# Top-k attention and GELU MLP in f32: the product of the last rows by column halves, scores of 512 in one matmul, preparation pieces spread in a slot

## The chip, the cores and the metric

One core of a Trainium2 chip runs the whole program. The metric is device time in microseconds (us), median of three runs. A separate, profiled execution gives the profile; in it, times are counted from the first instruction. The engines are TensorE (PE; its weight loads are listed as PEld), VectorE (DVE), ScalarE (ACT), GpSimd (POOL) and SyncE (SP), which issues most of the DMAs.

## The reference

Attention with a top-k mask, then an MLP with exact GELU. Shapes: batch 8, 8 heads, 576 rows, head size 64; the MLP goes 512 to 2048 to 512 for all 4608 rows. All of it is f32.

```python
scores = scale * np.matmul(q, k.transpose(0, 1, 3, 2))
kth = np.partition(scores, -32, axis=-1)[..., -32:-31]
scores = np.where(scores >= kth, scores, -1000000000.0)
attn = np.exp(scores - np.max(scores, axis=-1, keepdims=True))
attn = attn / (np.sum(attn, axis=-1, keepdims=True) + 1e-09)
x = np.matmul(attn, v)              # (B,H,S,D) -> (B*S, H*D)
h = x @ w_in
g = 0.5 * h * (1.0 + erf(h / sqrt(2)))
return g @ w_out
```

## The kernel before

**Items.** Heads are taken in pairs; a pair's q, k and v lie side by side in 128 columns (head e=0 in 0 to 63, e=1 in 64 to 127). The 576 rows of a head are four tiles of 128 (t = 0 to 3) and a last tile of 64 (t = 4, NM in the code). An item is one tile of both heads of a pair. The last 64 rows of two neighbouring pairs share an item, so a batch has 16 main items and 2 last items, 144 items in all. Even batches end with their last items and odd ones begin with them, so four last items come in a row: 16 to 19, 52 to 55, 88 to 91 and 124 to 127.

**Slots.** The loop at L616 works on several items at a time. Its pass n, called slot n here, issues in this order: `scores(n+2)`, `attend(n-3)` (product with v, for every second main item and every last item), the transposes of item n-2, both softmax halves of item n-1, and top-k of item n. Between them it puts pieces of the MLP (`mlp(1)`), eight in most slots. Every engine has its own queue and runs it in exactly the order in which the code issues; nothing reorders it.

**Scores** (L281). For a main item there is one matmul for the last 64 columns of both heads (L291) into the PSUM tile `t_ps`, and four (L295) into `s_ps`: two heads by two halves of 256 columns. The heads use rows 0 to 63 and 64 to 127 of the array. ACT copies both with a scale (L299, L300). For a last item four small matmuls (L305, 64 weight columns by 64) and four of 512 (L316) do the same.

**Softmax.** DVE finds the top 32 (L342, L345). POOL makes `neg` and `bias` of them (L357, L360). ACT applies Prelu with a steep slope (L381) and Exp with a running sum `den` (L382), once for each head e. POOL adds 1e-9 to `den` (L374), DVE takes its reciprocal `rden` (L368), inside top-k of the next item, and POOL normalises both heads (L393).

**Transposes** (L399) come as three pieces: `tails` (L410, or L415 for a last item) with the last 64 columns of both heads, then `main(0)` and `main(1)` with four 128x128 transposes each (L428). ACT copies each result out of PSUM (L411 or L420, L435).

**Product** (L441). For main items, 2 x 5 matmuls of 256 columns (L459) with 64 weight columns for each head: head e=0 writes PSUM partitions 0 to 63, e=1 writes 64 to 127. One ACT copy moves the result into `xT` (L464). For last items, 2 pairs x 5 matmuls (L469) use all 128 weight columns and 128 moving columns; a half of what they compute belongs to another head and isn't used, and two ACT copies take the other half (L475).

**Preparation** (L238). For each pair, ten 128x128 transposes of q and k (L250) come in three pieces of 4, 2 and 4, each followed by a copy into `qk`, nearly always on ACT (L254). The third (c = 0) also issues the loads of pair + 2 on SP. `slots_of` and `first` (L605 to L609) say in which slot each piece falls. Two fall in one slot in slot 2 and in slots 14, 15 and 16 of each 36.

**MLP pieces.** A piece is four matmuls' records of the first layer (L507, 256 columns) or two of the second (L543, 512 columns). They come in blocks of eight, an L2 block and an L1 block by turns. GELU_AT is 5: with the sixth piece of an L2 block ACT gets the two Gelus of the next blocks (L518). Gelu and Exp need different tables, so ACT loads a table (ACT_TABLE_LOAD) each time it goes from one to the other.

**PSUM.** `t_ps`, `o`, `tp`, `tp_t` and `tp_qk` share one tag with two buffers, used by turns in the order of issue: each new tile waits until the tile before the last has been copied out.

The order of a slot's second part is this:

```python
for piece in tr[:-1]:
    piece()
    ready[0] = n_tok[0]
    mlp(1)
...
if late:
    softmax(n - 1, 1)
add_small(n - 1)
for piece in tr[-1:] + prep_in.pop(n, []):
    piece()
    mlp(1)
```

Of the kernel before, what the change touches and what calls it, by code (L numbers as in the profile page):

```python
# [14 lines left out]
def kernel(  # L15
# [19 lines left out]
    nc = tc.nc  # L35
# [5 lines left out]
    B, H, S, D = q.shape  # L41
    P = 128
# [6 lines left out]
    TL = S - SM  # L49
    NJ = NM + 1  # L50
# [17 lines left out]
    xT = const.tile([P, KO, RING], f32, name="xT")  # L68
# [15 lines left out]
    def raw_of(n, pair):  # L84
        return raws[n][pair % len(raws[n])]

    def load(n, pair, queue=None):
        if pair >= n_pairs:
            return
        queue = queue or nc.sync  # L90
        b, h0 = pair // NP, 2 * (pair % NP)
        t, src = raw_of(n, pair), sources[n]
        for e in range(2):
            queue.dma_start(
                out=t[:, 0:NM, e, :], in_=src[b, h0 + e, 0:SM].rearrange("(t p) d -> p t d", p=P)
            )
            queue.dma_start(out=t[e * TL : (e + 1) * TL, NM, e, :], in_=src[b, h0 + e, SM:S])
# [28 lines left out]
    def unit_in(n):  # L126
        return ORDER[n - FIRST] if 0 <= n - FIRST < UNITS else None
# [66 lines left out]
    def weights_add(u):  # L194
        if u in words:
            w, _, dst = parts(u)
            d = dst.bitcast(i32)
            if on_pool(u):
                nc.gpsimd.tensor_scalar(
                    w.bitcast(i32), w.bitcast(u32), 2.0**-13, None, op0=ALU.mult  # L200
                )
            nc.gpsimd.tensor_tensor(d, d, w.bitcast(i32), op=ALU.add)
# [23 lines left out]
    def place_of(b, row):  # L226

        if row < SM:
            return b // 2 * RING + b % 2 * (SM + 2 * TL) + row
        return b // 2 * RING + SM + b % 2 * TL + row - SM  # L230
# [4 lines left out]
    KT = SM + 2 * P  # L235
# [32 lines left out]
    def spread(t, step, n):  # L268

        return bass.AP(tensor=t.tensor, offset=t.offset, ap=[list(t.ap[0]), [step, 2], [1, n]])  # L270

    def half(r, e):


        return slice((r ^ e) * TL, ((r ^ e) + 1) * TL)

    def halves(t, e, step):

        return spread(t[:, e * TL :], step + (TL if e == 0 else -TL), TL)

    def scores(i):  # L281
        if i >= N:
            return
        pair, t = items[i]
        S_of[i] = s = work.tile([P, 2 * S], f32, tag="s", bufs=5, name="s")
        s_ps = ps.tile([P, 2, 512], f32, tag="s", bufs=1, name="s_ps")
        t_ps = ps.tile([P, 512], f32, tag="tp", name="t_ps")
        if t < NM:
            qk = qk_of[pair]
            lhsT = qk[:, t * P : (t + 1) * P]  # L290
            nc.tensor.matmul(t_ps[:, 0:P], lhsT=lhsT, rhs=qk[:, SM + P : KT], start=True, stop=True)  # L291
            for c in range(2):
                for e in range(2):
                    rows = slice(e * D, (e + 1) * D)
                    nc.tensor.matmul(  # L295
                        s_ps[:, e, c * 256 : (c + 1) * 256], lhsT=lhsT[rows, :],
                        rhs=qk[rows, KT + c * 256 : KT + (c + 1) * 256], start=True, stop=True,
                    )
            nc.scalar.activation(spread(s, S + TL, SM), s_ps, func=AF.Copy, scale=scale)  # L299
            nc.scalar.activation(s[:, SM : S + TL], t_ps[:, 0:P], func=AF.Copy, scale=scale)  # L300
        else:
            for r in range(2):
                qk = qk_of[pair + r]
                for e in range(2):
                    nc.tensor.matmul(  # L305
                        t_ps[half(r, e), r * TL : (r + 1) * TL],
                        lhsT=qk[:, SM + e * TL : SM + (e + 1) * TL],
                        rhs=qk[:, SM + P + e * TL : SM + P + (e + 1) * TL],
                        start=True, stop=True,
                    )  # L310

            for r in range(2):
                qk = qk_of[pair + r]
                for e in range(2):
                    rows = slice(e * D, (e + 1) * D)
                    nc.tensor.matmul(  # L316
                        s_ps[half(r, e), r, :], lhsT=qk[rows, SM + e * TL : SM + (e + 1) * TL],
                        rhs=qk[rows, KT:], start=True, stop=True,
                    )
            s2 = s.rearrange("p (r n) -> p r n", r=2)  # L320
            nc.scalar.activation(s2[:, :, 0:SM], s_ps, func=AF.Copy, scale=scale)
            nc.scalar.activation(
                s2[:, :, SM:S], t_ps[:, 0:P].rearrange("p (r n) -> p r n", r=2),
                func=AF.Copy, scale=scale,
            )
# [115 lines left out]
    def attend(i):  # L441

        if i < 0 or i >= N:
            return False
        pair, t = items[i]
        b, at = divmod(pair, NP)
        if t < NM and t % 2 == 0:
            return False
        pt = pt_now[0]
        o = ps.tile([P, 512], f32, tag="tp", name="o")  # L450
        n, row = (2 * P, (t - 1) * P) if t < NM else (TL, SM)
        tok = place_of(b, row)
        assert read[0] >= tok + n - RING
        c = slice(tok % RING, tok % RING + n)
        if t < NM:
            vt = raw_of("v", pair)
            for j in range(NJ):
                for e in range(2):
                    nc.tensor.matmul(  # L459
                        o[e * D : (e + 1) * D, 0:n], lhsT=vt[:, j, e, :],  # L460
                        rhs=pt[:, e * NM + j if j < NM else 2 * NM, :],
                        start=(j == 0), stop=(j == NJ - 1),
                    )
            nc.scalar.copy(out=xT[:, at, c], in_=o[:, 0:n])  # L464
        else:
            for r in range(2):
                vt = raw_of("v", pair + r)
                for j in range(NJ):
                    nc.tensor.matmul(  # L469
                        o[:, r * P : (r + 1) * P], lhsT=vt[:, j].rearrange("p e d -> p (e d)"),  # L470
                        rhs=pt[:, r, j, :], start=(j == 0), stop=(j == NJ - 1),
                    )
            for e in range(2):
                r = slice(e * D, (e + 1) * D)
                nc.scalar.copy(out=xT[r, at : at + 2, c], in_=halves(o[r, 0 : 2 * P], e, P))  # L475

        if t == (NM if b % 2 == 0 else NM - 1):
            for r in range(2 if t == NM else 1):
                load("v", pair + r + NP + 1)
        if at == (NP - 1 if t < NM else NP - 2):  # L480
            assert n_tok[0] == tok
            n_tok[0] = tok + n
        return True
# [93 lines left out]
    def mlp(n):  # L577
        for _ in range(n):
            if done[0] >= len(pieces) or pieces[done[0]][0] > ready[0] or left[0] == 0:
                return  # L580
            pieces[done[0]][1]()
            done[0] += 1
            left[0] -= 1
# [26 lines left out]
    prep_in = {}  # L610
    for pair in range(2, n_pairs):
        b, p = divmod(pair, NP)
# [3 lines left out]
    for n in range(ahead):  # L616

        left[0] = 7 if START < n < START + 2 * NP else 8
        weights_add(unit_in(n))
        scores(n + 2)  # L620
        product = attend(n - 3)
        late = n > START + 1
        mlp(1)
        tr = transposes(n - 2)
        if product and done[0] < len(pieces) and pieces[done[0]][0] > ready[0]:

            for piece in tr[:1]:
                piece()
            tr, ready[0] = tr[1:], n_tok[0]
        softmax(n - 1, 0)  # L630
        mlp(1)
        if not late:
            softmax(n - 1, 1)
        mlp(1)
        for piece in tr[:-1]:
            piece()
            ready[0] = n_tok[0]
            mlp(1)
        ready[0] = n_tok[0]
        if late:  # L640
            softmax(n - 1, 1)
        add_small(n - 1)
        for piece in tr[-1:] + prep_in.pop(n, []):
            piece()
            mlp(1)
        mlp(left[0])
        if n < N:
            top_k(n, {3: lambda: inverse(n - 1)})
        else:
            inverse(n - 1)  # L650
        threshold(n)
        normalise(n - 1)

        weights_sign(unit_in(n))
        weights_size(unit_in(n + 1))
        if n >= FIRST:
            load_weights(n + 2)
        if n <= NP:
            load("v", n)
# [36 lines left out]
```

## Time and profile before

| what | value |
|---|---|
| median of 3 runs | 1690.68 us (1690.24 to 1690.70) |
| profiled execution, its own time | 1691.79 us |
| its span, first to last instruction | 1690.0 us |
| mean granted TensorE clock | 0.977 |
| L469 matmuls, 320 records | 40.0 us busy |
| L295 matmuls, 1024 records | 156.5 us busy |
| L459 matmuls, 1280 records | 155.1 us busy |
| L507 and L543 matmuls | 554.7 and 549.1 us busy |
| L250 transposes, 320 records | 61.2 us busy |

In the profile, the busy time of a group is the union of its instructions, so matmuls that run side by side are counted once. A matmul's listed duration is longer than the distance to the next one, since they are pipelined; the cost of one is read from start to start. An f32 matmul of the program appears as two records, a transpose as one. The lines of a timeline give start, length, engine, line, operation, out<-in, the array rows and columns that are used ("128*64"), the shape of the moving operand and the number of merged records, and in brackets the engine's idle time before and what ended it.

### The profile page before, as it was taken

What the parts mean: (1) busy time and instruction counts of PE and PEld (TensorE: products, weight loads), DVE (VectorE), ACT (ScalarE), POOL (GpSimd) and SP (SyncE); (2) the same over time, 40 slices, a digit from 0 to 9 for tenths busy, and PEclk for the clock granted to TensorE, in tenths of its full rate; (3) what the DMA queues carried; (4) which work ended last, traced back from release to release, by engine and by line L of the source; (5) the groups of instructions that cost most, each with busy time, mean ns of one, the idle gap of its engine ahead of it and who ended that gap; (6) DMA issues with size and microseconds to landing.
All of it is one profiled execution on the core that took longest, in us unless ns stands there. A gap on an engine that the chain in (4) does not pass through costs nothing.

```text
span 1690.0 us, 24403 instructions
## 1 busy us (share of the span) xinstructions
PE 1611.4 (95%) x8480; PEld 1093.3 (65%) x8480; DVE 1428.8 (85%) x3042; ACT 1188.1 (70%) x2147; POOL 662.5 (39%) x764
## 2 busy tenths in 40 slices
PE   5659899999999999999999999999999999999999
PEld 3336567676666667676666667676666666766665
DVE  6999798998889888998889888898889988899900
ACT  5778677777777777777777777777777777777730
POOL 3668743333333332333333333333333333333410
PEclk8669999999999999999999999999999999999999
DMA  6422210001100011002110111001110000000000
GB/s 158 135 91 98 78 48 9 11 18 35 29 27 15 27 29 41 1 13 49 25 31 1 35 36 41 1 14 28 32 46 1 27 15 15 21 1 13 7 13 13
DMA packets 126715, 56.10 MB, mean 33 GB/s; under 512 B 117888, under 2 KB 117888, under 8 KB 126592
## 3 DMA queue, kind: packets, MB, share of 16 engines
q1 hardware_dynamic: 125056, 52.16, 11.6%
q0 software_dynamic: 320, 2.10, 0.4%
q8 instruction: 67, 1.10, 0.3%
q14 instruction: 56, 0.46, 0.1%
q10 hardware_dynamic: 1216, 0.30, 0.1%
HBM read 45.08 MB, written 9.44 MB: 32 GB/s over the span
## 4 chain that ended last, share of the span: by engine, by line
PE 87%; ACT 5%; DVE 5%; POOL 1%; issue 1%; DMA 1%; SPq 0%; ACTq 0%; POOLq 0%
PE h_ps L507 29%; PE y_ps L543 28%; PE o L459 8%; PE s_ps L295 7%; PE tp L428 7%; DVE top L342 2%; PE o L469 2%; DVE rest L345 2%; PE tp_qk L250 2%; PE t_ps L291 2%; ACT s L382 1%; PE tp_t L410 1%; PE s_ps L316 1%; ACT s L381 1%; ACT L518 1%
## 5 line engine op out<-in xcount | busy, mean ns | idle before, releaser
L342 DVE MAX8 top<-rest 128x8 f32<-128x576 f32 x864 | 610.8, 750 | 0.0
L507 PE MATMUL h_ps<-xT,w_in_sb 128*128 128x256 f32 (+1 forms) x2560 | 554.7, 362 | 6.8 <-DMA xT<-in_moe_w_out_dram 4.9
L543 PE MATMUL y_ps<-w_out_sb,g 128*128 128x512 f32 x1152 | 549.1, 599 | 0.0
L393 POOL TENSOR_SCALAR s<-s,rden 128x576 f32<-128x576 f32 x288 | 493.5, 1723 | 0.8 <-issue 0.4
L507 PEld LDWEIGHTS h_ps<-xT,w_in_sb 128*128 128x128 f32 x2560 | 430.1, 191 | 69.4 <-issue 18.4
L345 DVE MATCH_REPLACE8 rest<-top,rest 128x576 f32<-128x576 f32 x576 | 424.3, 746 | 0.0
L374 POOL TENSOR_SCALAR den<-den 128x2 f32<-128x2 f32 x144 | 32.0, 222 | 868.7 <-ACT s L382 868.2
L543 PEld LDWEIGHTS y_ps<-w_out_sb,g 128*128 128x128 f32 x1152 | 195.4, 191 | 166.0 <-issue 164.6
L299 ACT ACTIVATE s<-s_ps 128x1024 f32<-128x1024 f32 x128 | 131.5, 1027 | 173.2 <-PE s_ps L295 153.0
L382 ACT ACTIVATE s<-s,bias 128x576 f32<-128x576 f32 x288 | 223.3, 776 | 13.2 <-ACT s L381 0.4
L381 ACT ACTIVATE s<-s,neg 128x576 f32<-128x576 f32 x288 | 223.7, 777 | 0.7 <-POOL neg L357 0.2
L435 ACT COPY pt<-tp 128x512 f32<-128x512 f32 x256 | 146.8, 575 | 98.2 <-PE tp L428 97.6
L345 DVE MATCH_REPLACE8 rest<-top,s 128x576 f32<-128x576 f32 x288 | 212.1, 746 | 0.0
L342 DVE MAX8 top<-s 128x8 f32<-128x576 f32 x288 | 202.2, 745 | 5.1 <-ACT s L300 5.1
L428 PEld LDWEIGHTS tp<-ident,s 128*128 128x128 f32 x1152 | 145.9, 144 | 93.3 <-issue 58.1
L428 PE MATMUL tp<-ident,s 128*128 128x128 f32 x1152 | 177.7, 278 | 6.4 <-ACT pt L411 6.4
L368 DVE RECIPROCAL rden<-den 128x2 f32<-128x2 f32 x144 | 23.6, 164 | 169.8 <-POOL den L374 169.5
L295 PE MATMUL s_ps<-qk 64*128 64x256 f32 x1024 | 156.5, 427 | 0.4 <-ACT s L299 0.4
L459 PE MATMUL o<-pt,raw_v 128*64 128x256 f32 x1280 | 155.1, 389 | 1.8 <-ACT pt L435 1.8
L459 PEld LDWEIGHTS o<-pt,raw_v 128*64 128x64 f32 x1280 | 87.5, 139 | 69.5 <-issue 15.1
L295 PEld LDWEIGHTS s_ps<-qk 64*128 64x128 f32 x1024 | 94.1, 198 | 24.3 <-issue 2.5
L518 ACT ACTIVATE g<-h_ps 128x512 f32<-128x512 f32 x144 | 78.7, 595 | 38.8 <-PE h_ps L507 38.0
(65 smaller groups left out, 1106.7 us busy)
## 6 DMA issues: line engine op xcount, KB each, us to landing
raw_q<-in_q_dram SPq DMA_DIRECT2D x64, 128.0 KB, 2.4
raw_v<-in_v_dram SPq DMA_DIRECT2D x64, 128.0 KB, 2.4
out_dram<-y SPq DMA_DIRECT2D x32, 256.0 KB, 2.2
raw_k<-in_k_dram SPq DMA_DIRECT2D x62, 128.0 KB, 2.4
w_out_sb<-in_moe_w_in_dram SPq DMA_DIRECT2D x12, 511.8 KB, 4.8
w_out_sb<-in_moe_w_out_dram SPq DMA_DIRECT2D x10, 511.8 KB, 3.9
w_out_sb<-in_moe_w_in_dram POOLq DMA_DIRECT2D x4, 511.8 KB, 7.7
words<-in_moe_w_out_dram SPq DMA_DIRECT2D x4, 511.8 KB, 6.5
```

What stands on the lines that cost most here:

```text
L295: nc.tensor.matmul(s_ps[:, e, c * 256 : (c + 1) * 256], lhsT=lhsT[rows, :], rhs=qk[rows, KT + c * 256 : KT + (c + 1) * 256], start=True, s ...
L299: nc.scalar.activation(spread(s, S + TL, SM), s_ps, func=AF.Copy, scale=scale)
L342: nc.vector.max(st["top"][:, e, 8 * r : 8 * r + 8], cur[e])
L345: nc.vector.match_replace(rest[:, e], st["top"][:, e, 8 * r : 8 * r + 8], cur[e], LOWEST)
L381: nc.scalar.activation(s, s, func=AF.Prelu, bias=st["neg"][:, e, 1:2], scale=1.0, alpha=STEEP)
L382: nc.scalar.activation(s, s, func=AF.Exp, bias=st["bias"][:, e : e + 1], scale=1.0, accum_out=st["den"][:, e : e + 1],)
L393: nc.gpsimd.tensor_scalar(s, s, st["rden"][:, e : e + 1], None, op0=ALU.mult)
L428: nc.tensor.transpose(tp[:, j * P : (j + 1) * P], s[:, first + j * P : first + (j + 1) * P], ident)
L435: nc.scalar.copy(out=dst, in_=tp.rearrange("p (j n) -> p j n", j=NM))
L459: nc.tensor.matmul(o[e * D : (e + 1) * D, 0:n], lhsT=vt[:, j, e, :], rhs=pt[:, e * NM + j if j < NM else 2 * NM, :], start=(j == 0), stop= ...
L507: nc.tensor.matmul(h_tile(u)[:, i, :], lhsT=w_in_sb[:, ko, f * P : (f + 1) * P], rhs=xT[:, ko, c0 : c0 + n], start=(ko == 0), stop=(ko == ...
L543: nc.tensor.matmul(y_of[sub], lhsT=g_of[u][:, i, sub * P : (sub + 1) * P], rhs=w_out_sb[:, f, :], start=(f == 0), stop=(f == FT - 1),)
```

## The change

There are three parts. The product of the last rows calls one matmul for each head, with 64 weight columns and the 64 moving columns of this head, into the partitions of this head; one copy replaces two. The scores of a main item take one matmul of 512 columns for each head instead of two of 256. In a slot with two or more preparation pieces and three transpose pieces, the first preparation piece is issued behind the first transpose piece, and the others stay at the end.

```diff
-            for c in range(2):
-                for e in range(2):
-                    rows = slice(e * D, (e + 1) * D)
-                    nc.tensor.matmul(
-                        s_ps[:, e, c * 256 : (c + 1) * 256], lhsT=lhsT[rows, :],
-                        rhs=qk[rows, KT + c * 256 : KT + (c + 1) * 256], start=True, stop=True,
-                    )
+            for e in range(2):
+                rows = slice(e * D, (e + 1) * D)
+                nc.tensor.matmul(
+                    s_ps[:, e, :], lhsT=lhsT[rows, :], rhs=qk[rows, KT:], start=True, stop=True
+                )
...
                 for j in range(NJ):
-                    nc.tensor.matmul(
-                        o[:, r * P : (r + 1) * P], lhsT=vt[:, j].rearrange("p e d -> p (e d)"),
-                        rhs=pt[:, r, j, :], start=(j == 0), stop=(j == NJ - 1),
-                    )
-            for e in range(2):
-                r = slice(e * D, (e + 1) * D)
-                nc.scalar.copy(out=xT[r, at : at + 2, c], in_=halves(o[r, 0 : 2 * P], e, P))
+                    for e in range(2):
+                        nc.tensor.matmul(
+                            o[e * D : (e + 1) * D, r * TL : (r + 1) * TL], lhsT=vt[:, j, e, :],
+                            rhs=pt[:, r, j, half(r, e)], start=(j == 0), stop=(j == NJ - 1),
+                        )
+            nc.scalar.copy(
+                out=xT[:, at : at + 2, c],
+                in_=o[:, 0 : 2 * TL].rearrange("p (r n) -> p r n", r=2),
+            )
...
         mlp(1)
+        prep = prep_in.pop(n, [])
+        if len(prep) > 1 and len(tr) == 3:
+            tr, prep = tr[:1] + prep[:1] + tr[1:], prep[1:]
         for piece in tr[:-1]:
             piece()
             ready[0] = n_tok[0]
...
-        for piece in tr[-1:] + prep_in.pop(n, []):
+        for piece in tr[-1:] + prep:
             piece()
             mlp(1)
```

## Prediction

> **What bounds the kernel now.** I read the page first, then busy time by stretch, then the timelines of single slots (a slot is one pass of the loop at L616, dated by the first matmul of `scores`), then the waits.
>
> ```profile
> PE 1611.4 (95%) x8480; PEld 1093.3 (65%) x8480; DVE 1428.8 (85%) x3042; ACT 1188.1 (70%) x2147; POOL 662.5 (39%) x764
> PE   5659899999999999999999999999999999999999
> PE 87%; ACT 5%; DVE 5%; POOL 1%; issue 1%; DMA 1%; SPq 0%; ACTq 0%; POOLq 0%
> ```
>
> TensorE (PE) is nearly always busy and carries 87% of the chain that ended last. By stretch it is sharper:
>
> ```profile
> 41.00:228.00 187.00, 138.06 (x711) 89.35 (x712) 173.07 (x348) 145.66 (x244) 134.31 (x102) 0.82 0.31 95
> 228.00:1600.00 1372.00, 1365.52 (x7361) 936.27 (x7362) 1224.80 (x2631) 997.86 (x1830) 506.51 (x625) 1.00 0.09 22
> ```
>
> The columns are span, PE, PEld, DVE, ACT, POOL, granted clock. From 228 to 1600 us PE lacks only 6.5 us, at full clock; all of it is six gaps: three of 1.27 us (ahead of 466.74, 862.44 and 1258.14, for the data of a last `qk` piece, which the change doesn't touch) and three of 0.85 us, ahead of 598.08, 993.78 and 1389.48. So in this stretch a microsecond of PE work is a microsecond of time, while DVE has 147 us and ACT 374 us to spare. But DVE and ACT follow PE slot by slot, so a new wait of PE for ACT counts in full too.
>
> **The product of the last rows (L469).** Slot 19, and two shapes from slot 52:
>
> ```profile
> 236.23 1.14 PE L295 MATMUL s_ps<-qk 64*128 64x256 f32 x8
> 237.30 2.50 PE L469 MATMUL o<-ptt,raw_v 128*128 128x128 f32 x20
> 239.63 2.74 PE L543 MATMUL y_ps<-w_out_sb,g 128*128 128x512 f32 x6
> ```
> ```profile
> 598.08 0.45 PE L305 MATMUL t_ps<-qk 128*64 128x64 f32 x8 [0.85 <-ACT qk L254]
> 598.46 1.09 PE L316 MATMUL s_ps<-qk 64*64 64x512 f32 x8
> 599.48 2.38 PE L459 MATMUL o<-pt,raw_v 128*64 128x256 f32 x20
> 601.79 0.70 PE L507 MATMUL h_ps<-xT,w_in_sb 128*128 128x256 f32 x2
> ```
>
> Every f32 matmul of the program is two records (10 calls of L469, x20). L469 takes 237.30 to 239.63, 2.33 us: 20 steps of 0.111 and 0.11 for its first weight load. Added are 20 calls, 40 records, of 64 columns, in two column halves. L305 has just this shape: read off in narrow windows its records start in pairs, 0.058 apart (598.18, 598.24, 598.30). So 20 pairs x 0.0585 = 1.17. The change of array shape around it is read at L459: 599.48 to 601.79 is 2.31 for 10 pairs of 256 columns at 0.216 (2.16), so 0.15 for the first load and the change behind; and L507 then starts with a step of 0.32 (0.70 less one duration of 0.38) where 0.22 is usual, 0.10 more. Today L469 has no such change behind it, as L543 uses the whole array too. After: 1.17 + 0.15 + 0.10 = 1.42. **Gain 0.91 us in each of the 16 last items, 14.6 us**, all on PE, in slots 19 to 22 of each 36, which have no gap. Two ACT copies of 0.26 become one of about 0.26 (L411 moves a 128x128 tile in 0.26): 16 x 0.26 = 4.2 us of ACT, off the path, counted as nothing. What is late next there: these slots shrink from 11.7 to 10.8 us while DVE needs 9.8 (busy in each of them), so DVE keeps 1 us; the normalise of POOL ends 3.5 us ahead of the transposes that read it (250.39 against 253.91), which leaves 2.6.
>
> The unknown is whether 80 instructions (40 records and 40 weight loads) can be supplied in 1.17 us, 15 ns each. L305 does 16 at that rate, and L316's 16 follow at once. For the sequencer itself: it passed the semaphore wait ahead of L428 at 192.9 and the one ahead of L507 at 193.1, with 8 instructions between: at most 25 ns each. Bounds per item are thus 1.17 and 80 x 25 = 2.00 us. I take 1.17, since the nearest row has the very shape and part of the burst is already queued when it starts.
>
> A rule speaks against this. The Trainium skill, "TensorE: Matmul & The Clock Gate", section "Wait — 56ns, not 53.3ns?", says that with hardware decode off the sequencer spends about 62 ns on each MATMUL, which then bounds short ones. By it the product would last an estimated 40 x 62 = 2.48 us and the whole change would end near 1703 us; L305's records, 29 ns each, do not agree, though for 8 of them only.
>
> **Scores (L295).** 128 items: four pairs of 256 columns become two of 512. Now start to start (236.23 to 237.30): 1.07 = 4 x 0.216 + 0.20 for first load and change. After: 2 x 0.428 (L543's step, its 6 records end 2.74 after the first start, 5 steps and one duration of 0.60) + 0.20 = 1.06. Gain 0.007 x 128 = **0.9 us**. If the halves stopped running side by side it would cost 0.86 an item; L316 (8 records of 512, four abreast, in 1.09) excludes that. Half the weight loads go as well, hidden under matmuls: nothing.
>
> **Preparation spread.** Two pieces fall in slot 2 and in slots 14, 15, 16 of each 36. The first now runs right after the `tails` piece, so it and one more `mlp` piece stand ahead of `softmax(n-1,1)` in the order of PE and ACT. No work is added; three things move.
>
> (a) ACT makes the `qk` copy (0.59 or 0.37, next piece 1.3 later) ahead of the softmax, so `den` is 1.3 us later. In slot 50 the normalise then ends at about 590.2; `tails` of slot 51 is at 590.91. Covered by 0.7; slot 52 likewise, by 0.8. If that cover is gone it costs up to 0.6 each. The loads of `piece` c=0 that are now issued earlier go to SP, which has nothing due.
>
> (b) In slots 51, 87, 123 the extra `mlp` piece is the sixth of an L2 block, and that is the one that carries the Gelu (GELU_AT). Today:
>
> ```profile
> 592.52 0.59 ACT L435 COPY pt<-tp 128x512 f32<-128x512 f32 x1 [1.03 <-PE tp L428]
> 593.00 0.78 ACT L381 ACTIVATE s<-s,neg 128x576 f32<-128x576 f32 x1
> ...
> 594.59 0.56 ACT L435 COPY pt<-tp 128x512 f32<-128x512 f32 x1
> 595.17 1.28 ACT L518 ACT_TABLE_LOAD   x1
> ...
> 597.43 1.08 ACT L254 COPY qk<-tp_qk 128x512 f32<-128x512 f32 x2
> ```
>
> Order now: first `main` copy, softmax, second `main` copy, Gelu, both `qk` copies; the next `t_ps` needs the PSUM buffer that the first `qk` copy frees at 598.02, hence the gap of 0.85. Afterwards: `tails`, `qk`, first `main` (593.81 to 594.40), Gelu, softmax with a second table load, second `main`, `qk`; and the next `t_ps` waits for the second `main`. Slot 17 already shows that order:
>
> ```profile
> 217.92 1.28 ACT L518 ACT_TABLE_LOAD   x1
> ...
> 220.19 0.59 ACT L435 COPY pt<-tp 128x512 f32<-128x512 f32 x1
> 220.66 0.80 ACT L381 ACTIVATE s<-s,neg 128x576 f32<-128x576 f32 x1
> 221.47 1.28 ACT L382 ACT_TABLE_LOAD   x1
> ...
> 223.54 0.56 ACT L435 COPY pt<-tp 128x512 f32<-128x512 f32 x1
> ```
>
> From the table load to the end of the second copy: 224.10 - 217.92 = 6.18, less 0.47 for the copy inside, 5.7. From 594.4 that is 600.1; so the matmuls of 598.08 start at 600.15, with a gap of 3.0 us (PE is ready at 597.2). **Loss 2.1 us x 3 = 6.3.** Queued behind the late softmax on ACT are the copies that PE waits for; `den` slips from 594.76 to 599.7, so DVE's reciprocal, and DVE behind it, is 5 us late; normalise ends near 603.9, and the shifted `tails` is at 606.6, so nothing more is lost.
>
> (c) Slot 15 has its Gelu earlier and other ACT work; by the same bookkeeping the second `main` copy ends 0.8 us after the present start of slot 16: 0.8 lost. Slot 2 waits for DVE and POOL in either order: 0.
>
> **Sum:** -14.6 - 0.9 + 6.3 + 0.8 = -8.4. Against the profiled execution (1691.79; span 1690.0) that is 1683.4; the median of the runs is 1.1 lower, so **1682.3**.
>
> **Rivals.**
> B, the spreading is free: if ACT isn't in the order I derived, so that Gelu stays behind the softmax, only (a) remains, -15.5, 1675.2; with the three gaps of 0.85 gone too, 1672.6. For: PE had waits behind `qk` copies, which are now apart. Against: slot 17. Chance 0.14.
> C, the spreading costs more: the covers of 0.7 and 0.8 fail in some nine slots at 0.5 each, or DVE's 5 us come back as waits for POOL: +4.5, 1686.8 (1684 to 1689). For: margins under 1 us; against: DVE gains about 1 us a slot afterwards. Chance 0.16.
> D, slower: supply of instructions to PE in the product. At 25 ns, 2.00 us each, the gain falls to 0.08 an item: -1.3 - 0.9 + 7.1 = +4.9, 1695.6. It turns the sign from about 21 ns on (gain 0.39 an item, burst of 1.69). Against it, L305. Chance 0.12, a little over half of it at under 21 ns.
> E, the change doesn't do what it says: the halves run one behind the other, 40 x 0.0585 = 2.34, +0.25 = 2.59 against 2.33: +4.2 - 0.9 + 7.1, 1701. L305 and L459 speak against. Chance 0.04.
> My case: 0.52, 1680.5 to 1685; unnamed 0.02.
>
> **Range.** 1674.5 to 1688.5 holds my case, most of B, nearly all of C and a third of D, a little over 8 in 10. This kernel's times tell 0.2% (3.4 us) from no change. Faster by more (under 1687.3): 0.52 + 0.14 + 0.10 of C + 0.04 of D = 0.80; within: 0.06 + 0.03, 0.09; slower: 0.05 + 0.04 + 0.02 = 0.11.
>
> **What would show it.** The new product: 40 records of 128x64, first start to next piece near 1.3 us, slots 19 to 22 at 10.8 us. The gaps ahead of slots 52, 88, 124 near 3.0 us and laid to the second `main` copy, with two table loads between it and the first. L295 at 4 records, 1.06. A product of 1.7 us or more, or slots 52 without a gap, would make me wrong.

## The result and the profile after

The changed kernel takes 1686.94 us (median of 6 runs, 1686.40 to 1690.16) against 1690.69 of before: ratio 0.9983, interval 0.997 to 0.9996. It is a little faster, by 3.75 us where 8.4 were forecast. The profiled execution took 1686.40 us with a span of 1684.6, against 1691.79 and 1690.0: 5.4 less. Slot by slot this 5.4 can be told exactly, so I work with it; the median of before lies 1.1 under its profiled execution and the median of after 0.5 above.

Lines of the changed kernel have other numbers: L294 scores, L468 product of last rows, L303 and L314 scores of last items, L457 product of main items, L426 and L433 the `main` transposes and copies, L379 and L380 Prelu and Exp.

The head of its page, and busy time in the two stretches (span, PE, PEld, DVE, ACT, POOL, granted clock, DMA):

```profile
PE 1596.2 (95%) x8288; PEld 1024.6 (61%) x8288; DVE 1428.5 (85%) x3042; ACT 1181.9 (70%) x2131; POOL 662.5 (39%) x764
PE 86%; DVE 6%; ACT 5%; POOL 1%; issue 1%; DMA 1%; SPq 0%; ACTq 0%; POOLq 0%
```
```profile
41.00:228.00 187.00, 135.97 (x658) 81.28 (x656) 171.79 (x346) 145.19 (x242) 133.20 (x101) 0.82 0.30 94
228.00:1600.00 1372.00, 1358.98 (x7267) 881.00 (x7267) 1228.48 (x2639) 995.60 (x1821) 508.45 (x630) 1.00 0.09 22
```

PE is busy 15 us less in all, but from 228 to 1600 us it now lacks 13.0 us in place of 6.5. The product is where it was expected (timeline of slot 19):

```profile
236.49 1.13 PE L294 MATMUL s_ps<-qk 64*128 64x512 f32 x4
237.55 1.39 PE L468 MATMUL o<-ptt,raw_v 128*64 128x64 f32 x40
238.87 1.55 PE L543 MATMUL y_ps<-w_out_sb,g 128*128 128x512 f32 x3
```

237.55 to 238.87 is 1.32 us for 40 records. Slots 19 to 22 take 10.76, 10.80, 10.76 and 10.69 us in place of 11.68, 11.72, 11.68 and 11.61, each 0.92 less, and so do their three repeats.

Slot 51 is where time comes back. Its timeline on ACT:

```profile
590.26 0.59 ACT L433 COPY pt<-tp 128x512 f32<-128x512 f32 x1 [0.71 <-PE tp L426]
590.87 1.28 ACT L518 ACT_TABLE_LOAD   x1
592.16 1.09 ACT L518 ACTIVATE g<-h_ps 128x512 f32<-128x512 f32 x2
593.13 0.78 ACT L379 ACTIVATE s<-s,neg 128x576 f32<-128x576 f32 x1
593.92 1.28 ACT L380 ACT_TABLE_LOAD   x1
595.22 0.77 ACT L380 ACTIVATE s<-s,bias 128x576 f32<-128x576 f32 x1
...
595.99 0.56 ACT L433 COPY pt<-tp 128x512 f32<-128x512 f32 x1
```

Gelu and two table loads stand between the two `main` copies, 590.87 to 596.55, 5.7 us, and PE waits for the second. The timeline of PE after it, and the granted clock by microsecond (the column behind POOL's):

```profile
596.61 0.45 PE L303 MATMUL t_ps<-qk 128*64 128x64 f32 x8 [2.93 <-ACT pt L433]
596.99 1.09 PE L314 MATMUL s_ps<-qk 64*64 64x512 f32 x8
598.01 4.07 PE L457 MATMUL o<-pt,raw_v 128*64 128x256 f32 x20
```
```profile
597.00:598.00 1.00, 1.00 (x11) 0.20 (x8) 1.00 (x4) 0.04 (x1) 1.00 (x1) 1.00 0.00 0
598.00:599.00 1.00, 1.00 (x10) 0.68 (x8) 1.00 (x3) 0.80 (x1) 1.00 (x2) 0.64 0.00 0
599.00:600.00 1.00, 1.00 (x8) 0.52 (x6) 1.00 (x3) 0.40 (x2) 1.00 (x1) 0.50 0.00 0
...
602.00:603.00 1.00, 1.00 (x7) 0.89 (x6) 1.00 (x3) 0.88 (x2) 0.00 (x0) 1.00 0.00 0
```

The gap of 2.93 us is the one that was forecast. What follows was not: from 598.28 on TensorE gets half its clock for 3.41 us, and the main product, 2.38 us elsewhere, takes 4.07. PE counts as busy in it, so no wait and no gap shows this; it is seen in the clock, in the time of L457's matmuls and in the length of the slot. The same table by slots, for the three places:

```profile
596.61:610.76 14.15, 14.15 (x84) 10.06 (x84) 10.48 (x23) 7.33 (x15) 4.65 (x8) 0.88 0.01 1
...
992.26:1004.72 12.46, 12.46 (x83) 9.27 (x83) 10.48 (x23) 7.33 (x15) 4.64 (x8) 1.00 0.00 1
...
1386.23:1400.33 14.10, 14.10 (x83) 9.64 (x83) 10.48 (x23) 7.33 (x15) 4.64 (x8) 0.88 0.00 1
```

Same slot, same instructions: 12.46 us at full clock (as before the change), 14.15 and 14.10 where the clock was halved. The whole account against the profiled execution of before:

| where | us |
|---|---|
| product, 16 x 0.92 | -14.7 |
| gaps ahead of slots 52, 88, 124: 3 x 2.08 | +6.2 |
| half clock in slots 52 and 124: 1.69 + 1.64 | +3.3 |
| scores and what is left behind slot 19 | -0.5 |
| up to slot 19 (235.92 to 236.18) | +0.3 |
| sum | -5.4 |

### The profile page after: what moved, and what is told of

Read it like the earlier page. It is cut to its first block, busy times and chain, and to the rows that moved or that the text cites. A ratio compares the mean times of both kernels' runs of the same rounds, so it can differ in the third digit from the quotient of the medians.

```text
span 1684.6 us, 23982 instructions
## 1 busy us (share of the span) xinstructions
PE 1596.2 (95%) x8288; PEld 1024.6 (61%) x8288; DVE 1428.5 (85%) x3042; ACT 1181.9 (70%) x2131; POOL 662.5 (39%) x764
## 4 chain that ended last, share of the span: by engine, by line
PE 86%; DVE 6%; ACT 5%; POOL 1%; issue 1%; DMA 1%; SPq 0%; ACTq 0%; POOLq 0%
PE h_ps L507 30%; PE y_ps L543 28%; PE o L457 8%; PE s_ps L294 7%; PE tp L426 7%; DVE top L340 3%; DVE rest L343 3%; PE tp_qk L250 2%; PE t_ps L291 2%; PE o L468 1%; PE tp_t L408 1%; PE s_ps L314 1%; ACT s L380 1%; POOL s L391 1%; ACT L518 1%
## 5 line engine op out<-in xcount | busy, mean ns | idle before, releaser
L380 ACT ACTIVATE s<-s,bias 128x576 f32<-128x576 f32 x288 | 223.4, 776 | 13.2 <-ACT s L379 0.4
L379 ACT ACTIVATE s<-s,neg 128x576 f32<-128x576 f32 x288 | 224.0, 778 | 0.3 <-POOL neg L355 0.2
L433 ACT COPY pt<-tp 128x512 f32<-128x512 f32 x256 | 146.7, 574 | 100.6 <-PE tp L426 100.6
L426 PEld LDWEIGHTS tp<-ident,s 128*128 128x128 f32 x1152 | 146.5, 144 | 92.1 <-issue 59.2
L426 PE MATMUL tp<-ident,s 128*128 128x128 f32 x1152 | 177.8, 279 | 6.0 <-ACT pt L409 5.9
L457 PE MATMUL o<-pt,raw_v 128*64 128x256 f32 x1280 | 157.8, 394 | 1.9 <-ACT pt L433 1.8
L294 PE MATMUL s_ps<-qk 64*128 64x512 f32 x512 | 153.3, 677 | 0.4 <-ACT s L297 0.4
L457 PEld LDWEIGHTS o<-pt,raw_v 128*64 128x64 f32 x1280 | 88.6, 141 | 95.9 <-ACT qk L254 19.9
```

Source lines behind the costliest of these rows:

```text
L294: nc.tensor.matmul(s_ps[:, e, :], lhsT=lhsT[rows, :], rhs=qk[rows, KT:], start=True, stop=True)
L379: nc.scalar.activation(s, s, func=AF.Prelu, bias=st["neg"][:, e, 1:2], scale=1.0, alpha=STEEP)
L380: nc.scalar.activation(s, s, func=AF.Exp, bias=st["bias"][:, e : e + 1], scale=1.0, accum_out=st["den"][:, e : e + 1],)
L426: nc.tensor.transpose(tp[:, j * P : (j + 1) * P], s[:, first + j * P : first + (j + 1) * P], ident)
L433: nc.scalar.copy(out=dst, in_=tp.rearrange("p (j n) -> p j n", j=NM))
L457: nc.tensor.matmul(o[e * D : (e + 1) * D, 0:n], lhsT=vt[:, j, e, :], rhs=pt[:, e * NM + j if j < NM else 2 * NM, :], start=(j == 0), stop= ...
```

## The experiments

The theory: each part does what was forecast, and the spreading costs more than its gaps, since the gaps slow the clock. The rivals: the new product or scores leave slower slots behind; or the long slots come from queues on ACT or DVE.

**Product alone** (e1_product; scores and preparation as before the change).

> The product by heads alone, with the scores and the order of preparation of before. Theory (the changed kernel is short of its forecast only by what the spreading costs, gaps and a slowed clock): slots 19 to 22 of each 36 at 10.8 us in place of 11.7, 16 x 0.92 = 14.7 us less, 1676.0; the three gaps ahead of 598, 993 and 1389 stay at 0.85 and the clock stays full behind them. Rival (the new product itself leaves PE in a state in which other slots are slower, for one by its change of array shape): some of slots 52, 88, 124 are again some 1.7 us longer, and the time is 1679 or more.

1676.5 us, ratio 0.992 (0.9903 to 0.9936). Slots 55 to 58 take 10.76, 10.80, 10.76 and 10.69; the gaps stay at 0.84 to 0.85, and the clock is full from 200 us to the end. Theory holds; the new shape leaves nothing slow behind.

**Scores alone** (e2_scores; only L295 is replaced by one matmul of 512 for each head).

> The scores by one matmul of 512 alone. Forecast of the prediction: 0.007 us an item, 0.9 us less, 1689.8. By the slots of the changed kernel it is rather 0.004 us an item, 0.5 us less, 1690.2. Rival (fewer weight loads and instructions help PE elsewhere, or 512 columns in two banks hold up the copies): 2 us or more either way. No slot should differ by more than 0.02 us after 230 us.

1690.89 us, ratio 1.0001 (0.9991 to 1.001): no difference that the medians can show. In the trace slots 50 to 85 take 395.58 us in place of 395.71, 0.004 for each of their 32 main items, or 0.5 us in all.

**Spreading alone** (e3_spread).

> The spreading of the preparation alone. Theory: three gaps of 2.9 us in place of 0.85 ahead of slots 52, 88, 124, +6.2 us, and behind some of them 3.4 us of half clock, +1.7 us each: 1697 without, 1702 with all three; with some change of up to 1.5 us before 230 us. Rival (the spreading is free and the forecast was missed elsewhere): within 1 us of before. Rival (the long slots 52 are due to queues of ACT or DVE and not to the clock): they are long in all three places or in none, and the granted clock is 1.00 in them.

1703.6 us, ratio 1.0079 (1.0064 to 1.0094): alone it makes the kernel slower. The three gaps are 2.93 us, and this time all three slots behind them are slowed:

```profile
598.99:613.09 14.10, 14.10 (x84) 9.96 (x84) 10.48 (x23) 7.34 (x15) 4.65 (x8) 0.88 0.00 1
998.41:1012.51 14.10, 14.10 (x83) 9.92 (x83) 10.48 (x23) 7.35 (x15) 4.65 (x8) 0.88 0.00 0
1397.84:1411.94 14.10, 14.10 (x84) 9.92 (x84) 10.48 (x23) 7.34 (x15) 4.65 (x8) 0.88 0.00 0
```

3 x (2.08 + 1.64) = 11.2, and from slot 19 to slot 141 the profiled execution takes 11.15 us more than that of before. The medians differ by 12.9; where the other 1.7 lie isn't shown, since this profiled execution was 1.2 us shorter ahead of slot 19. ACT's and DVE's busy time in these slots is what it is in the undisturbed slot of the changed kernel (7.33 and 10.48), so queues on them are not the reason.

**Product and scores, no spreading** (e4_product_scores).

> The changed kernel without the spreading. Theory: 14.7 and 0.5 us less, 1675.5, which is faster than both kernels; gaps of 0.85 as before, clock full from 230 us on. Rival (the parts hinder one another, so that their sum is not the parts' sum): 1679 or more.

1675.6 us, ratio 0.9914 (0.9899 to 0.9929), as the theory had it, and faster than both kernels. Slots 50 to 85 take 391.9 us; the changed kernel needs 395.65 for them. The profiled executions of the two differ by 10.9 us: 6.2 by the gaps, 3.3 by the half clock, 1.5 ahead of slot 19. The medians differ by 11.3.

**The changed kernel with the Gelu one piece later** (e5_after_gelu6).

```diff
-    GELU_AT = 5
+    GELU_AT = 6
```

> The changed kernel with GELU_AT = 6, so that in slots 51, 87 and 123 the Gelu comes behind the softmax again, though the preparation is spread. Theory (the loss is the Gelu and two table loads ahead of the softmax): no gap ahead of slot 52, at most 1 us ahead of its product, which then waits for the last qk copy; no slowed clock; 1676 if nothing else moves with the constant. Rival (the loss is from the preparation pieces themselves, whatever Gelu does): gaps near 2.9 us stay, 1685 to 1690.

1672.48 us, ratio 0.9889 (0.9874 to 0.9904). With spreading and all, the gaps ahead of slots 52, 88 and 124 are gone, and so is the slow clock; ahead of the product PE waits 0.74:

```profile
592.85 0.45 PE L303 MATMUL t_ps<-qk 128*64 128x64 f32 x8
593.23 1.09 PE L314 MATMUL s_ps<-qk 64*64 64x512 f32 x8
595.06 2.38 PE L457 MATMUL o<-pt,raw_v 128*64 128x256 f32 x20 [0.74 <-ACT qk L254]
```

So it is the Gelu's place relative to the softmax that makes most of the spreading's cost, not the preparation pieces. It is also faster than expected: the three gaps of 1.27 us, which I had laid to a last `qk` piece, are gone too. There, too, the Gelu stood ahead of the `qk` copy that PE waits for (before: Gelu from 463.83, copy at 466.09, matmuls at 466.74); now the copy, at 461.20, comes ahead of the Gelu, at 462.66.

**Spreading only in slots with a product** (e6_spread_even).

```diff
-        if len(prep) > 1 and len(tr) == 3:
+        if product and len(prep) > 1 and len(tr) == 3:
```

> The changed kernel with the spreading only in slots with a product (14 and 16 of each 36), and not in slots 2 and 15, 51, 87, 123. Theory: spreading costs nothing there, the gaps are 0.85 as before, 1675.5, like product and scores without spreading. Rival (later softmax in slots 50 and 52 costs waits for the normalise of POOL, up to 0.6 us in seven slots): up to 1680.

1676.96 us, ratio 0.9913 (0.9897 to 0.993). Slots 50 and 52 take 12.46 as before: a softmax 1.3 us later costs nothing there. The covers of 0.7 and 0.8 us hold. From slot 19 to slot 141 it takes 1324.19 us, and e4_product_scores without any spreading 1324.22, so behind slot 19 the whole price of the spreading comes from slots 51, 87 and 123.

**The gap shorter by one piece** (e7_gap_short; one MLP piece moved from behind the gap to ahead of it).

```diff
+        if n > 2 * START and n % 36 in (15, 16):
+            left[0] = 9 if n % 36 == 15 else 7
```

> The changed kernel with one MLP piece (0.86 us of PE) moved from slots 52, 88, 124 to the end of the slots before them; nothing else changed. Theory (an idle stretch of nearly 3 us is what halves the clock): gaps of 2.07 us in place of 2.93, granted clock 1.00 in all three slots; 3 x 0.86 = 2.6 us less by the gaps and the share of slowed slots less: about 1682. Rival (the slow slots have another cause, such as queues behind the late softmax): two of three slots still 1.7 us long, 1684.4.

1685.97 us, ratio 0.9968 (0.9956 to 0.998). The gaps are 2.07 us, as planned, but two of the three slots are slowed again:

```profile
595.62:609.09 13.47, 13.36 (x79) 9.42 (x79) 9.80 (x22) 6.83 (x15) 4.06 (x6) 0.87 0.01 1
991.15:1002.93 11.78, 11.67 (x79) 8.62 (x79) 9.80 (x22) 6.83 (x15) 4.06 (x6) 1.00 0.01 1
1384.98:1398.41 13.43, 13.31 (x80) 9.08 (x80) 9.81 (x22) 6.84 (x15) 4.06 (x6) 0.87 0.00 1
```

My expectation that 2.07 us is too short to slow the clock was wrong. It is the clock, by its column, and not queues, since ACT and DVE are as busy in the slowed slots as in the other (6.83 and 9.80); but a shorter gap is enough. (A wait of 0.35 for POOL in slot 54 comes with the moved piece: it stands in e11_gap_shorter too, and in no other trace.)

**The gap longer by one piece** (e8_gap_long; 7 and 9 in the same two lines).

> The changed kernel with one MLP piece moved the other way, from slots 51, 87, 123 to the slots behind the gap. Theory: gaps of 3.79 us, half clock for 3.4 us behind every one of the three, each slot some 2.6 to 3.4 us longer than in before: 2.6 us more by the gaps and 1.7 more for each slot that wasn't slowed already, 1690 to 1692. Rival (the gap has nothing to do with the clock): slowed slots in some places only, as now.

1692.4 us, ratio 1.0008 (0.9998 to 1.0017). Gaps of 3.79 us, and all three slots are slowed, as the theory had it: two take 14.96 and 14.97 us, and one is slowed for two stretches of 3.41 us (16.30), which it did not have.

**The gap shorter by two pieces** (e11_gap_shorter; 10 and 6).

> The changed kernel with two MLP pieces moved from slots 52, 88, 124 into the slots before them. Gaps of 1.2 us in place of 2.93 (2.07 with one piece). Theory, mended by the last run (the clock is halved when over about half of a fixed stretch of 3.4 us is idle, so a gap of 2.07 does it by chance and one under 1.7 never): granted clock 1.00 in all three slots, no slot of 3.4 us more; about 1681 by the gaps alone, give or take a microsecond for pieces that are now missing between the copies of slot 52. Rival (any gap over 1 us that follows the late softmax slows these slots): slots 52 and 124 at half clock again, 1684 or more.

1682.96 us, ratio 0.9957 (0.994 to 0.9973). Gaps of 1.20 us, and the clock is full in all three:

```profile
596.68:608.46 11.78, 10.80 (x76) 7.91 (x76) 9.80 (x22) 6.83 (x15) 4.05 (x6) 1.00 0.01 1
990.50:1002.28 11.78, 10.80 (x75) 7.90 (x75) 9.80 (x22) 6.83 (x15) 4.05 (x6) 1.00 0.01 1
1384.31:1396.09 11.78, 10.80 (x75) 7.90 (x75) 9.80 (x22) 6.83 (x15) 4.05 (x6) 1.00 0.01 1
```

The price is a new gap of 0.98 at the end of the slot, where the two pieces are missing between the transposes, so the gain comes from the clock alone: slots 51 and 52 together take 25.11 us, as in the undisturbed case of e7_gap_short (13.33 + 11.78).

**No spreading, and the Gelu one piece later** (e10_ps_gelu6).

> Product and scores as in the changed kernel, no spreading, GELU_AT = 6. Theory (with the Gelu behind the softmax the spreading has nothing to give): in slots 51, 87, 123 the Gelu now stands between the two qk copies, the scores of the next slot don't wait, its product waits about 0.1 us in place of 0.74; some 2 us faster than the same with the spreading (1672.5), 1670.5, and the fastest of all. Rival (the spreading is worth something once the Gelu is out of its way): over 1672.5.

1668.88 us, ratio 0.9871 (0.9856 to 0.9886), the fastest of all. No gap over 0.3 us is left between 230 and 1600 us. Slot 52 takes 12.52 us where the spreading has 13.27: even with the Gelu behind the softmax the spreading costs 0.75 in each of the three places.

**No spreading, and the Gelu two pieces later** (e12_ps_gelu7).

> Product and scores without spreading, GELU_AT = 7: the Gelu behind both qk copies. Theory: no wait ahead of slots 52, 88, 124 at all, but the L1 piece that needs the Gelu's buffers comes one piece sooner, and in slots without a product there is no cover for it: 1670 if it stays covered everywhere, up to 1 us more in each slot where it isn't. Rival: the place of the Gelu behind the sixth piece makes no difference, 1670.5 as with 6.

1673.75 us, ratio 0.9902 (0.9887 to 0.9916), over 3 us more than either forecast. Slots 52, 88 and 124 wait no more (12.46 us), as the theory had it. From slot 19 to slot 141 it takes the same time as with 6, within 0.2 us (4 slots are 0.09 longer); at the end it loses 0.85 (a wait of 1.18 for the Gelu), and 3.3 us in the profiled executions lie ahead of slot 19, where the clock is unsteady. What part of these 3.3 is due to the constant stays open.

## Why the prediction was wrong

**The bound.** Right: from 230 us on, PE's time and the waits of PE for ACT are the time, to 0.2 us (before, 6.36 of the 6.48 us that PE lacks up to 1600 are the six gaps; after, 12.60 of 12.77).

**The product.** Right: 1.32 us from first start to the next piece, gain 0.92 where 0.91 was forecast. The 40 records start in pairs 0.058 apart to the end, so the supply of 80 instructions (rival D) was no limit. The rule of the Trainium skill that I weighed ("TensorE: Matmul & The Clock Gate", "Wait — 56ns, not 53.3ns?") doesn't bind here: a record takes 29 ns over 40 in a row, and not 62. The rule is for hardware decode off, and no run shows how that was set. Rival E is out as well.

**The scores.** Right in kind, 0.5 for 0.9 us; both are too small for the medians.

**The spreading, (a) and (c).** (a) right, by e6_spread_even. (c) was 0.8; up to slot 19 the profiled executions differ by 0.3, and that stretch varies from 234.24 to 239.28 us between the kernels, so it is not settled.

**The spreading, (b): the step that failed.** The order of ACT, the 5.7 us and the gap of 3.0 (2.93) were right, 6.2 for 6.3 us. But I priced the gap at its own length and took the slot behind it for unchanged. In two of three places a gap of this length halved TensorE's clock for 3.41 us, 1.64 to 1.69 us more each: +3.3 on a sum of -8.4, a term that I had left at nothing. With this term, and the small ones, the sum is -5.4, what the profiled execution shows. That slot 88 escaped is chance: it depends on where the gap falls on a fixed grid, as the last section shows. The medians differ by only 3.75; of the 1.6 that remain, 1.1 is the distance of before's median from its profiled execution, which I took over, and 0.5 that of after.

The row that would have told me was on the table: I showed 41 to 228 us with a granted clock of 0.82, and this is the stretch in which PE has gaps of up to 4.9 us. A clock of 1.00 afterwards was not a property of the stage but of its having no gap over 1.27 us; and my own forecast put three gaps of 3.0 into it. The Trainium skill says so, too ("TensorE: Matmul & The Clock Gate", "Why this matters for your kernels": no idle gaps over about 3 us between bursts of matmuls); here gaps of 2.07 us were enough in two cases of three, and one of 2.93 was not, so less is enough and the length alone does not decide.

**Rivals.** The time fell where rival C had it (1686.8), but by luck, not for its reason: no cover of POOL's failed. Rival B was wrong; the spreading is the only part that costs.

## What to carry to other kernels

Where TensorE is the bound and its clock is full, price a new wait twice: by its length, and, from about 1.5 us on (an estimate, 45% of the 3.41 us step described below), by the slower clock that may follow; look at the granted clock of stretches of the same trace that already have such gaps. When work is moved within a slot, follow what is issued along with it: here not the moved transposes but the Gelu hung on an MLP piece, with two table loads, crossed the softmax, and PE waited for what stood behind. A change of several parts is worth taking apart: the product alone gives 14 us, the scores nothing, and the spreading takes back most of it.

## What the runs showed of the hardware

The granted clock changes in steps of 3.41 us (half clock lasts 3.41, 6.83, 10.24 us and so on), on a grid that doesn't depend on the gap. In the changed kernel it falls at 598.28 and again at 1386.76 us, 788.48 apart, which is 231 steps of 3.4133 us. Behind nine of the ten gaps that slowed slots 52, 88 or 124 it fell 0.5 to 1.7 us after the gap's end, behind the tenth (e8_gap_long, slot 52) 0.5 before it. What decides is how much of the grid's last step PE was idle (without a matmul record), worked out from gaps and clock changes of the traces:

| kernel, slot | gap, us | most idle step before | half clock |
|---|---|---|---|
| changed, 52 | 2.93 | 1.74 of 3.41 (51%) | 3.41 us |
| changed, 88 | 2.93 | 1.48 (43%), the next 1.45 | none |
| changed, 124 | 2.93 | 2.88 (84%) | 3.41 us |
| e7_gap_short, 52 | 2.07 | 1.83 (54%) | 3.41 us |
| e7_gap_short, 88 | 2.07 | 1.42 (42%), the other 0.65 | none |
| e7_gap_short, 124 | 2.07 | 2.07 (61%) | 3.41 us |
| e8_gap_long, 52 | 3.79 | 3.27 (96%) | 6.83 us |

The other two gaps of e8_gap_long (70% and 86%) and the three of e3_spread (64 to 68%) brought one step of half clock each.

So the same gap costs 1.7 us more or nothing, by where it falls on the grid. Over all thirteen traces, the early stretch included, the clock never went to half behind a step with less than 45% idle (e6_spread_even, at 45.35 us) and always did above 59%; between the two it went either way (e12_ps_gelu7 kept full clock at 103.31 us behind 59%). It came back to full only behind a step with at most 17% idle (e12_ps_gelu7, at 52.11), and not always then (before, at 44.67, stayed at half behind 5%). That fits the early gaps, which are close to one another: in before the clock stays at half for 27.31 us from 31.02 on. From 240 us on, single gaps of 0.74 to 1.27 us never slowed it.

To find such a stretch, look at durations: TensorE's busy share hides it (PE is 100% busy in the slow slots), but the time of a group that occurs everywhere, L457's 20 records in 4.07 us where 2.38 are usual, shows it at once.
